# A fused attention and gated feed-forward kernel: new order and filler in the first batch, V projected behind the sums in the second

## The chip, the cores and the metric

The kernel runs on one core of a Trainium2 chip. Times are device microseconds of one execution; a span is the same execution from its first to its last instruction, some 1.8 us shorter. An execution counts as fast when it is within 1.5% of the fastest of its kernel.

PE is the matrix engine (PEld its weight loads), DVE the vector engine, ACT the scalar engine, POOL is GpSimd, SP the engine that issues the other transfers.

## The reference

```python
# batch 8, heads 8, sequence 1024, head size 64; E and F project the sequence to 64
k_proj = einsum('ks,bhsd->bhkd', E, k);  v_proj = einsum('ks,bhsd->bhkd', F, v)
scores = q @ k_proj.T / 8
attn = exp(scores - max);  attn = attn / (sum(attn) + 1e-9)
x = (attn @ v_proj) as [8192 tokens, 512]
out = (sigmoid(x @ w_gate) * (x @ w_val)) @ w_out          # 512 -> 1536 -> 512
```

## The kernel before

Nearly all of the time is the feed-forward part, "dense work": for each half batch of 512 tokens twelve pairs of matmul groups (gate into one bank of PSUM, value into another), then output projections. The attention of the next batch is put between them, in numbered slots. Only the first batch's attention has nothing to hide behind. It is done in half units with filler matmuls in the gaps, whose results nobody reads:

```python
def busy(n):                       # filler: keeps PE going
    for _ in range(n):
        mm(FB[3], bank[FB[3]][:, 0:P], ident[:, :], ident[:, :], ["ident"])
# ...
start_loads(); constants(); project_consts()
busy(6)
k_part(0); busy(3); turn_k(whole, 0); busy(6); k_part(1); busy(3)   # K: project, keep, turn
qt(0, ("DVE", "ACT")); turn_k(whole, 1)                             # Q turned on PE
sc(0)                                                               # first scores and exp
qt(1, ("DVE", "DVE")); busy(6)
den(0)                                                              # first sums, reciprocal, split
sc(1)                                                               # second scores and exp
busy(4); v_part(0); den(1)
bc(0); busy(4); xo(0); busy(6)                                      # spread, attention output -> xT
v_part(1); bc(1)
load_q(1); load_k(1); load_v(1)                                     # issued by POOL
# ... then dense work; xo(1) behind its first group
```

The order of the calls is the order on each engine. `whole` is a fixed list of the PSUM banks that these calls take; whoever uses a bank again waits for its last reader. After the sums, DVE takes the reciprocal and splits it into two bf16 parts, which the "spread" matmuls bring to all partitions:

```python
dve(reciprocal(rden, bank))                    # L593 here, L783 in the second batch
dve(tensor_copy(rhi, rden))                    # L594: cast to bf16
dve(scalar_tensor_tensor(rhl, rhi, -1, rden))  # L596: the rest
```

The second batch (b == 1) has the same parts in slots 12 to 24:

```python
return [k_alone, lambda: turn_k(att), v_alone, lambda: sc(0), lambda: sc(1),
        lambda: (den(), rec(0, ...)), lambda: rec(1, ...), lambda: rec(2, ...), lambda: rec(3, ...),
        split, lambda: bc(0), lambda: bc(1), lambda: xo(0), lambda: xo(1)]
spots = (12, 13, 14, 15, 16, 17, 18, 19, 20, 20, 21, 22, 23, 24)
```

The softmax here doesn't subtract the row's maximum and nothing guards it: scores larger than these inputs give would overflow.

Of the kernel before, what the change touches and what calls it, by code (L numbers as in the profile page):

```python
# [118 lines left out]
def bass_linformer_attn__then__ffn_glu_sigmoid_kernel(  # L119
# [18 lines left out]
    with contextlib.ExitStack() as es:  # L138
# [52 lines left out]
        class Ring:  # L191
# [8 lines left out]
        A0, A1, A2, A3 = AB  # L200
        F0, F1, F2, F3 = FB
        whole = Ring(
            (A0, A1, A2, A3, F0)
            + (A0, A1, F1, F2, A2)
            + (A3, F0, F1)
            + (A0, A1, A3, F0)
            + (A2, F2, A0, A1, F1)
            + (A3, A2, A0, A1, A3, A2)
        )
        ffn, att = Ring(FB), Ring(AB)  # L210

        def mm(b, o, lhsT, rhs, r, start=True, stop=True, tp=None, tr=False):
            kw = {}
            if tp is not None:
                kw["tile_position"] = tp
            if tr:
                kw["is_transpose"] = True
            else:
                kw["start"], kw["stop"] = start, stop
            return add("PE", lambda e: e.matmul(o, lhsT, rhs, **kw), r=r, x=[("bank", b)])  # L220
# [5 lines left out]
        def dve(fn, r, w, b=None):  # L226
            x = [] if b is None else [("bank", b)]
            return add("DVE", fn, r=r, w=w, x=x)
# [218 lines left out]
        def busy(n):  # L447
            for _ in range(n):
                mm(FB[3], bank[FB[3]][:, 0:P], ident[:, :], ident[:, :], ["ident"])
# [47 lines left out]
        def turn_k(ring, R=None):  # L497
            bk = ring.next()
            ob = bank[bk][:, :].bitcast(BF16)
            rs = range(NR)[pairs(R)]  # L500
            for n, r in enumerate(rs):
                for g in range(2):
                    mm(
                        bk,
                        ob[64 * g : 64 * g + 64, n * P : (n + 1) * P],
                        kp[:, r, :],
                        ident[:, :],
                        [("kp", r // 2), "ident"],
                        tr=True,
                        tp=(0, 64 * g),  # L510
                    )
            act(
                kpD[:, 2 * rs[0] : 2 * rs[-1] + 2, :].rearrange("p h c -> p (h c)"),
                ob[:, 0 : P * len(rs)],
                [],
                [("kpD", x) for x in both(R)],
                b=bk,
            )
# [153 lines left out]
        def attention(b):  # L672
# [60 lines left out]
            def sc(r2):  # L733
                for r in (2 * r2, 2 * r2 + 1):
                    bks = [att.next(), att.next()]
                    for c in range(2):
                        h = 2 * r + c
                        for g in range(2):
                            gg, oo = slice(64 * g, 64 * g + 64), 64 * (g ^ c)
                            mm(  # L740
                                bks[g],
                                bank[bks[g]][oo : oo + 64, :],
                                kpD[gg, h, :],
                                qT[s][gg, h, :],
                                [("kpD", r // 2), ("qT", s, r)],
                                tp=(64 * g, oo),
                            )
                    for g in range(2):
                        act(
                            eT[:, 2 * r + g, :],  # L750
                            bank[bks[g]][:, :],
                            [],
                            [("eT", 2 * r + g)],
                            b=bks[g],
                            func=AF.Exp,
                            scale=SCALE,
                        )

            def den():
                bk = att.next()  # L760
                for rnd in range(2):
                    for j in range(4):
                        n = 4 * rnd + j
                        mm(
                            bk,
                            bank[bk][32 * j : 32 * j + 32, :],
                            dsel[:, n % 2, rnd, :],
                            eT[:, n, :],
                            [("dsel", n % 2), ("eT", n)],
                            start=(rnd == 0),  # L770
                            stop=(rnd == 1),
                            tp=(0, 32 * j),
                        )
                if b == 1:
                    den_bank.append(bk)
                else:
                    for c in range(4):
                        rec(c, bk)

            def rec(c, bk):  # L780
                cc = slice(c * P, (c + 1) * P)
                dve(
                    lambda e: e.reciprocal(rden[:, cc], bank[bk][:, cc]),  # L783
                    [],
                    [("rden", c, R) for R in range(2)],
                    b=bk,
                )
# [77 lines left out]
            if b == 1:  # L865
                return [
                    k_alone,
                    lambda: turn_k(att),
                    v_alone,
                    lambda: sc(0),  # L870
                    lambda: sc(1),
                    lambda: (den(), rec(0, den_bank[0])),
                    lambda: rec(1, den_bank[0]),
                    lambda: rec(2, den_bank[0]),
                    lambda: rec(3, den_bank[0]),
                    split,
                    lambda: bc(0),
                    lambda: bc(1),
                    lambda: xo(0),
                    lambda: xo(1),  # L880
                ]
# [104 lines left out]
        start_loads()  # L986
        constants()
        project_consts()
        busy(6)
        qt, sc, den, bc, xo = half_unit(0, whole)  # L990

        def k_part(R):
# [7 lines left out]
            keep_v(bks, 0, ["ACT"] * 4, R)  # L1000

        k_part(0)
        busy(3)
        turn_k(whole, 0)
        busy(6)
        k_part(1)
        busy(3)
        qt(0, ("DVE", "ACT"))
# [1 line left out]
        sc(0)  # L1010
        qt(1, ("DVE", "DVE"))
        busy(6)
        den(0)
        sc(1)
        busy(4)
        v_part(0)
        den(1)
        bc(0)
        busy(4)
        xo(0)  # L1020
        busy(6)
        v_part(1)
        bc(1)
        load_q(1)
# [18 lines left out]
        for b in range(B):  # L1043
            todo = []
            for blk in (2 * b, 2 * b + 1):
                ms = [[m] for m in range(NF)]
                if blk <= 1:
                    ms = [[0, 1]] + ms[2:]
                if blk == 1:
                    gaps = {11: [0, 1, 2, 3]}  # L1050
                else:
                    gaps = {2: [0], 5: [1], 8: [2], 11: [3]}
                for m in ms:
                    if len(m) == 2:
                        todo.append(
                            lambda blk=blk: first_pair(blk, None if blk else lambda: xo(1))
                        )
                    else:
                        todo.append(lambda blk=blk, m=m[0]: mstep(blk, m))
                    if blk >= 1:  # L1060
                        for tt in gaps.get(m[-1], ()):
                            todo.append(lambda blk=blk, tt=tt: oproj(blk - 1, tt, ffn.next()))
            at = {}

            def put(i, fn):
                at.setdefault(i, []).append(fn)

            if b == 0:
                qt2, sc2, den2, bc2, xo2 = half_unit(1, att)
                put(4, lambda: (qt2(0, ("DVE", "ACT")), qt2(1, ("DVE", "ACT"))))  # L1070
                put(5, lambda: (sc2(0), sc2(1)))
                put(6, den2)
                put(8, lambda: (bc2(0), bc2(1)))
                put(9, lambda: (xo2(0), xo2(1)))
                spots = (12, 13, 14, 15, 16, 17, 18, 19, 20, 20, 21, 22, 23, 24)
            else:
                spots = (3, 6, 10, 13, 16, 16, 20, 23, 26, 29)
            if b + 1 < B:
                for i, fn in zip(spots, attention(b + 1)):
                    put(i, fn)  # L1080
            def load_next(n):
                load_k(n)
                load_q(n)
                load_v(n)

            if b == 0:
                put(16, lambda: load_next(2))
                put(24, lambda: transpose_q(2))
            else:
                if b + 2 < B:  # L1090
                    put(4, lambda b=b: load_next(b + 2))
                    put(20, lambda b=b: transpose_q(b + 2))
            for i, slot in enumerate(todo):
                slot()
                for fn in at.get(i, ()):
                    fn()
            assert max(at, default=0) < len(todo)
# [33 lines left out]
```

## Time and profile before

| | before |
|---|---|
| median of 3 executions | 568.17 us (567.77 to 569.35) |
| the execution that was traced | 569.20 us, span 567.4 us |
| PE busy | 550.5 of 567.4 us, 97% |
| waits of PE after its start | 1.2 us for rhl (second batch), 1.4 us for xT in all, 1.0 us for K |
| first Q half landed, clock at full rate, dense work begins | 13.2, 14.15, 22.4 us |

The 22.4 us are the first weight load (22.37), since the record of the first matmul is missing from this trace; one of the waits for xT is overstated by that.

With PE at 97% the places to look at are PE's waits, and for each wait the engine that ends it. The lines are in the prediction. One mark is used below: the start of the third pair of groups of dense work ("third pair").

### The profile page before, as it was taken

The numbers are of one execution on the slowest core, as the hardware profiler recorded it, in microseconds if no ns is written. First come the engines' busy times: TensorE is split into PE (matmuls) and PEld (weight loads), VectorE is DVE, ScalarE is ACT, GpSimd is POOL, SyncE is SP. The second block draws the span as 40 slices with busy tenths as digits, with TensorE's granted clock in tenths as the row PEclk, the third lists the DMA queues.
The fourth block names the chain that finished last, engine by engine and source line by source line (L and its number), as shares of the span: only waits on it lengthen the run. The fifth ranks groups of instructions, "written<-read, shape, count | busy, mean of one in ns | idle before, by whom it ended". The sixth has DMA issues, their size and how long they took to land.

```text
span 567.4 us, 7629 instructions
## 1 busy us (share of the span) xinstructions
PE 550.5 (97%) x2963; PEld 247.0 (44%) x3018; DVE 249.5 (44%) x397; ACT 177.4 (31%) x314; POOL 107.2 (19%) x148
## 2 busy tenths in 40 slices
PE   5899999999999999999999999999999999999998
PEld 4444434444444444444444444444444444444444
DVE  4544464353623545235443256334462354633332
ACT  2644632432143322352223422243214332222220
POOL 9400201007200080002600054000700007000000
PEclk9999999999999999999999999999999999999999
DMA  9999999936944059512677046560601001010112
GB/s 162 198 201 201 140 212 167 208 79 115 146 84 96 21 113 183 93 47 62 117 141 121 24 105 107 121 103 37 114 18 48 37 22 39 37 37 20 38 38 92
DMA packets 76564, 56.00 MB, mean 99 GB/s; under 512 B 34704, under 2 KB 68240, under 8 KB 76528
## 3 DMA queue, kind: packets, MB, share of 16 engines
q0 software_dynamic: 33984, 29.89, 34.8%
q1 hardware_dynamic: 42544, 25.63, 18.1%
q8 instruction: 23, 0.38, 0.3%
q14 instruction: 13, 0.11, 0.1%
HBM read 60.29 MB, written 16.78 MB: 136 GB/s over the span
## 4 chain that ended last, share of the span: by engine, by line
PE 95%; DVE 1%; DMA 1%; issue 1%; ACT 0%; POOL 0%; DVEq 0%; POOLq 0%
PE pF L220 88%; PE pA L220 7%; DMA KV<-in_k_dram 1%; DVE xT L645 1%; DVE hT L940 0%; DVE rden L783 0%; DVE rhl L794 0%; ACT qT L224 0%; DVE rhi L792 0%; POOL quad L313 0%; DVE ost L971 0%; DVEq L102 0%; POOLq L1116 0%
## 5 line engine op out<-in xcount | busy, mean ns | idle before, releaser
L940 DVE SCALAR_TENSOR_TENSOR hT<-sig,pF 128x512 bf16<-128x512 f32 x192 | 130.8, 685 | 200.0 <-PE pF L220 145.1
L224 ACT ACTIVATE sig<-pF 128x512 f32<-128x512 f32 x192 | 114.4, 599 | 318.3 <-PE pF L220 315.9
L220 PE MATMUL pF<-xT,wV 128*128 128x512 bf16 x753 | 196.2, 379 | 1.1 <-DVE hT L940 0.3
L220 PE MATMUL pF<-xT,wG 128*128 128x512 bf16 x746 | 194.4, 379 | 2.8 <-issue 1.3
L220 PE MATMUL pF<-wO,hT 128*128 128x512 bf16 (+2 forms) x762 | 173.9, 376 | 1.5 <-issue 0.8
L220 PEld LDWEIGHTS pF<-wO,hT 128*128 128x128 bf16 x780 | 74.7, 98 | 92.6 <-issue 6.2
L220 PEld LDWEIGHTS pF<-xT,wV 128*128 128x128 bf16 x768 | 75.1, 98 | 91.1 <-DVE hT L940 0.8
L220 PEld LDWEIGHTS pF<-xT,wG 128*128 128x128 bf16 x768 | 72.2, 98 | 95.3 <-issue 12.3
L829 POOL PARTITION_BROADCAST rb<-rrow x96 | 70.7, 798 | 217.1 <-DMA rrow<-rden 212.0
L971 DVE TENSOR_SCALAR ost<-pF 128x512 f32<-128x512 f32 (+1 forms) x65 | 44.4, 684 | 103.5 <-PE pF L220 103.4
L224 ACT ACTIVATE eT<-pA 128x512 bf16<-128x512 f32 x63 | 32.7, 606 | 8.4 <-PE pA L220 8.4
L854 DVE TENSOR_TENSOR xT<-pA,rb 128x512 bf16<-128x512 f32 x56 | 34.7, 682 | 0.0
L783 DVE RECIPROCAL rden<-pA 128x128 f32<-128x128 f32 x28 | 24.1, 916 | 0.0
L238 POOL DMA_DIRECT2D KV<-in_v_dram x9 | 7.8, 872 | 83.9 <-PE pF L220 83.9
L220 PE MATMUL pA<-KV,EFT 128*64 128x512 bf16 (+2 forms) x168 | 16.0, 332 | 1.0 <-DMA KV<-in_k_dram 1.0
L224 ACT ACTIVATE kpd<-pA 64x1024 bf16<-64x1024 f32 x6 | 6.1, 1017 | 28.3 <-PE pA L220 28.3
L238 POOL DMA_DIRECT2D KV<-in_k_dram x9 | 8.0, 889 | 32.3 <-PE pF L220 32.2
L220 PEld LDWEIGHTS pA<-KV,EFT 128*64 128x64 bf16 x168 | 8.3, 115 | 8.6 <-issue 3.4
L224 ACT ACTIVATE vpD<-pA 64x512 bf16<-64x512 f32 (+2 forms) x22 | 10.2, 465 | 2.2 <-PE pA L220 1.7
L220 PE MATMUL pA<-qT,kpD 64*64 64x512 bf16 (+1 forms) x140 | 10.4, 367 | 0.0
L220 PE MATMUL pA<-eT,vpD 64*64 64x512 bf16 (+1 forms) x140 | 10.4, 367 | 0.0
L238 POOL DMA_DIRECT2D Qb<-in_q_dram x11 | 9.4, 865 | 0.0
(69 smaller groups left out, 89.5 us busy)
## 6 DMA issues: line engine op xcount, KB each, us to landing
out_dram<-ost SPq DMA_DIRECT2D x63, 256.0 KB, 2.1
Qb<-in_q_dram POOLq DMA_DIRECT2D x7, 1024.0 KB, 15.6
KV<-in_k_dram POOLq DMA_DIRECT2D x7, 1024.0 KB, 11.0
KV<-in_v_dram POOLq DMA_DIRECT2D x7, 1024.0 KB, 10.5
wO<-in_moe_w_out_dram POOLq DMA_DIRECT2D x1, 1536.0 KB, 12.0
wG<-in_moe_w_gate_dram POOLq DMA_DIRECT2D x5, 256.0 KB, 18.4
wV<-in_moe_w_val_dram POOLq DMA_DIRECT2D x5, 256.0 KB, 19.0
KV<-in_k_dram POOLq DMA_DIRECT2D x2, 512.0 KB, 8.8
```

The source lines that it names most:

```text
L220: return add("PE", lambda e: e.matmul(o, lhsT, rhs, **kw), r=r, x=[("bank", b)])
L224: return add("ACT", lambda e: e.activation(o, i, func, scale=scale), r=r, w=w, x=x)
L238: add("POOL", lambda e: e.dma_start(o, i), r=r, w=w, dma=sem)
L645: lambda e, g=g, o=o: e.tensor_tensor(o, bank[bks[g]][:, :].rearrange("p (r c) -> p r c", r=2), rb[:, 2 * R + g, :].rearrange("p (r c) -> ...
L783: lambda e: e.reciprocal(rden[:, cc], bank[bk][:, cc]),
L829: lambda e, n=n, i=2 * rnd + c, j=j, parts=parts: e.partition_broadcast(rb[0:parts, n, :], rrow[32 * j : 32 * j + 1, i, :], channels=parts),
L854: lambda e, r=r, g=g, n=n, bk=bks[g]: e.tensor_tensor(xT[s][:, r, :, 256 * g : 256 * g + 256], bank[bk][:, :].rearrange("p (f c) -> p f c" ...
L940: lambda e: e.scalar_tensor_tensor(hT[blk % 2][:, m, :], sg[:, :], 1.0, bank[pv][:, :], ALU.add, ALU.mult,),
L971: lambda e, pb=pb, c0=c0, c1=c1: e.tensor_scalar(o[:, c0:c1], bank[pb][:, 0 : c1 - c0], 0.5, None, op0=ALU.mult),
```

## The change

The intent: turn PE's clock up earlier with more filler ahead of K, take the second scores out from behind the first sums, free the second spread of a busy bank, and give the second batch's reciprocals one slot more by moving V behind the sums.

```diff
         whole = Ring(
             (A0, A1, A2, A3, F0)
             + (A0, A1, F1, F2, A2)
-            + (A3, F0, F1)
-            + (A0, A1, A3, F0)
-            + (A2, F2, A0, A1, F1)
-            + (A3, A2, A0, A1, A3, A2)
+            + (A3, F0, A0, A1, F1)
+            + (A3, F0, A2)
+            + (F2, A0, A1, F1)
+            + (A3, A2, F2, A0, A3, A2)
         )
@@ second batch
-                    v_alone,
                     lambda: sc(0),
                     lambda: sc(1),
                     lambda: (den(), rec(0, den_bank[0])),
                     lambda: rec(1, den_bank[0]),
                     lambda: rec(2, den_bank[0]),
+                    v_alone,
                     lambda: rec(3, den_bank[0]),
@@ start
-        busy(6)
+        busy(18)
         k_part(0)
-        busy(3)
+        busy(4)
         turn_k(whole, 0)
-        busy(6)
+        busy(10)
@@
         busy(6)
+        sc(1)
         den(0)
-        sc(1)
@@
         xo(0)
-        busy(6)
+        busy(3)
@@
-                spots = (12, 13, 14, 15, 16, 17, 18, 19, 20, 20, 21, 22, 23, 24)
+                spots = (12, 13, 14, 15, 16, 17, 18, 18, 19, 19, 21, 22, 23, 24)
```

## The prediction

> **What bounds the kernel now.** I read the page first, then the waits of PE, then the timeline of PE and DVE around the two places that the change touches, then the landing times of the loads. The page says how much there is to win at all:
>
> ```profile
> span 567.4 us, 7629 instructions
> PE 550.5 (97%) x2963; PEld 247.0 (44%) x3018; DVE 249.5 (44%) x397; ACT 177.4 (31%) x314; POOL 107.2 (19%) x148
> PE   5899999999999999999999999999999999999998
> PE 95%; DVE 1%; DMA 1%; issue 1%; ACT 0%; POOL 0%; DVEq 0%; POOLq 0%
> ```
>
> PE is busy for 97% of the span, and the only slices below 90% are the first two and the last. 567.4 - 550.5 = 16.9 us are all that PE is idle. So no reordering can win over 3% unless it also makes matmuls shorter. The waits of PE, the whole span, tell where those idle times are:
>
> ```profile
> PE pA L220 <- DMA EF<-in_F_dram: 5.8, 1, 5.8
> PE pF L220 <- issue: 2.1, 13, 0.2
> PE pA L220 <- DVE rhl L794: 1.2, 1, 1.2
> PE pA L220 <- DMA KV<-in_k_dram: 1.0, 1, 1.0
> PE pF L220 <- DVE xT L645: 0.9, 3, 0.5
> PE pA L220 <- DVE xT L645: 0.5, 1, 0.5
> ```
>
> The columns are total us, times, longest. The 5.8 us at the start wait for E and F and are not touched. Two lines are what the change aims at: 1.2 us for rhl (L794, the second batch) and the waits for xT (L645, the first). The second batch in the timelines, PE then DVE:
>
> ```profile
> 72.88 1.03 PE L220 MATMUL pF<-xT,wV 128*128 128x512 bf16 x4
> 75.15 0.39 PE L220 MATMUL pA<-rhl,bsel 32*128 32x512 bf16 x4 [1.24 <-DVE rhl L794]
> ...
> 72.28 0.69 DVE L940 SCALAR_TENSOR_TENSOR hT<-sig,pF 128x512 bf16<-128x512 f32 x1 [0.17 <-PE pF L220]
> 72.89 0.95 DVE L783 RECIPROCAL rden<-pA 128x128 f32<-128x128 f32 x1
> 73.88 0.43 DVE L792 CAST rhi<-rden 128x512 bf16<-128x512 f32 x1
> 74.34 0.75 DVE L794 SCALAR_TENSOR_TENSOR rhl<-rhi,rows,rden 128x512 bf16<-128x512 bf16 x1
> ```
>
> The fourth reciprocal and the split run on DVE after a gate (72.28) and end at 75.09; the broadcast matmuls that need them could have begun at 73.84. And the start of the kernel:
>
> ```profile
> 13.89 0.43 DVE L549 COPY qT<-pA 128x512 bf16<-128x512 bf16 x1 [7.17 <-PE pA L220]
> 18.94 0.96 DVE L593 RECIPROCAL rden<-pA 64x128 f32<-64x128 f32 x1 [0.42 <-PE pA L220]
> 20.97 0.69 DVE L645 TENSOR_TENSOR xT<-pA,rb 128x512 bf16<-128x512 f32 x1
> 21.58 0.68 DVE L645 TENSOR_TENSOR xT<-pF,rb 128x512 bf16<-128x512 f32 x1
> ...
> L220 PE MATMUL pF<-KV,EFT x24: 219/314/316, 11.9 to 17.9; 128*64 128x128 bf16 x24
> ```
>
> Dense work (the gate and value matmuls) begins when xT is ready, at 22.4 us, and DVE's chain of sums, split and xT is what comes last. The last line (min/median/max ns) shows one matmul shape at two speeds, 314 ns early and 219 ns later. In the timeline, sixteen of them take 1.06 us at 9.35 and at 11.92, and 0.64 us at 20.32; the turn from slow to fast lies between 13.3 and 14.2 us. The row PEclk of the page reads 9 in every slice and does not show it.
>
> [...] 128-column matmuls start 107 ns apart early and 56 ns apart later[...]; this kernel waits by whole bank, and the trace shows it: the second spread waits 0.50 us for "DVE xT L645", a reader of the old contents of its bank A1, although its own data (rhl) are there at 20.94.
>
> **The change part by part.** Both kernels do the same useful work; only filler is added (18+4+10+3 in place of 6+3+6+6 at the four places changed, so 14 more on PE) and order moves.
>
> (a) Second batch. Slots are one pair of gate and value groups each, 1.73 us of PE (8 x 0.216). Before, V (16 matmuls, 0.89 us) comes after slot 14, scores after 15 and 16, sums after 17, reciprocals after 17 to 20, spread after 21. Now scores after 14 and 15, sums and first reciprocal after 16, V after 18, the fourth reciprocal and the split after 19, spread still after 21. The PE work ahead of the spread is the same, so PE gets there at 73.84 again in the old time frame (72.88 + 4 x 0.216 + 0.1 for the change of tile). When is rhl there? V's matmuls now end near 68.6; ACT copies vpD for 1.58 us (59.73 to 61.31 in the old trace), so until 70.2; then sigmoid 19, 0.6, to 70.8; gate 19 on DVE, 0.69, to 71.5; reciprocal 0.95 (its row), 72.45; cast 0.43; split 0.75; ready at about 73.65. That is 0.2 us before PE asks. So the wait goes whole: 75.15 - 73.84 = **1.3 us**, of which 0.2 us of margin is thin. Gates 20 and 21 come 1 us later on DVE, but the four matmuls groups behind them are output projections of the half batch before, whose inputs are long there.
>
> (b) First batch, the clock. The 12 extra fillers run in the wait for K: 18 x 0.107 = 1.93 us from 7.5, so to 9.43 where K was begun at 9.35; a cost of 0.1 us that later slack takes up (0.2 us of waiting before the second K half at 11.92). They make PE busy without a gap from about 7.3 on[...]. What gets faster on the path: the first Q half lands at 13.2 (issued at 2.98, 10.2 us to landing), so nothing before that moves the end. From there the eight transposes of Q take 0.62 in place of 1.03: **0.4 us**.
>
> (c) First batch, second scores ahead of the first sums. They stood behind sums that waited for exp (16.09 to 16.90). Now they follow the copies of qT directly: with (b), exp of the second scores ends near 17.5 in place of 18.44. V's first half lands at 17.0 and is not hurried; the second sums come at 17.5 to 17.9. DVE finishes the first split at 18.1, the second reciprocal runs 18.15 to 19.1, second split done at 20.05, xT from 20.1 to 21.4. Dense work begins near 21.5 against 22.4: **0.9 us**, (b) included.
>
> (d) Other banks for the second spread (F2, A0 for A0, A1). Their readers end by 20.6, so it runs at 20.4 to 20.7, not at 21.7. The second spread's copies then start after vpD (V's second half lands at 19.65, copies to about 21.6), and the second xT ends near 23.7, against 24.79. So the matmuls that need all of xT start near 23.8 in place of 24.93: **1.1 us** for (b), (c) and (d) together. The new bank F2 is also the third group's of the first pair; it is asked for near 22.7 and read out by 22.2, so no wait.
>
> Sum: 1.3 + 1.1 = 2.4 us if both come whole.
>
> **The rivals.** 1. The saved time turns into a wait for a load. For: loads fill the first 60 us (DMA row at 9). Against, by landing times: first weights 20.3 to 22.4 for 21.5 to 24.3; wV of the fourth chunk 33.1 against 35.3 less 1.1; transposed Q of batch 1 in four parts from 55.6 to 58.7, while the first scores now ask near 57.5 for two parts landed by 56.4 and the second near 60 for the rest; wO lands at 71.3 and is asked for near 73. The margins are 1 to 2 us: this could eat some tenths. Total near 566.5. 2. The clock does not turn earlier[...]. Then sc(1) still moves, by 0.5 us, and dense work by 0.3 to 0.4: total gain 1.3 + 0.4 = 1.7, 566.5. 3. V's copies on ACT (1.58 us) delay the gate that the last reciprocal stands behind, by more than I count; margin 0.2 us. If they cost 0.5 more, the second batch gains only 1.0. 4. ACT becomes the bound of the start: its queue of exp, vpD and rb is in one order, and V's landings fix two points of it. Then the gain of (b) to (d) is 0.5, total 566.4.
>
> **Range and chances.** 568.17 - 2.4 = 565.8. Weighing the rivals (each some tenths, all one way) I take 2.1 off: 566.1. The runs before spread over 1.6 us (567.77 to 569.35)[...]; the low end, 565.0, needs both gains whole and a good draw; the high end, 567.5, is a gain under 0.7. 2% would be 11.4 us, more than two thirds of PE's whole idle time, so faster or slower by that much would need something I don't see.
>
> **What would show each step.** (a): the wait "DVE rhl L794" of 1.2 gone from PE's waits, rhl done before slot 21 ends. (b): matmuls of 219 ns for the second K half at 11.9. (c): first xT matmul near 21.5. (d): no wait of PE for "DVE xT L645" ahead of the second spread. From 100 us on all must be the old trace, moved earlier by one constant amount. It is wrong if that amount is under 0.7 us, if PE waits for KV, qT, w or wO, or if anything after 100 us changes.

The forecast's sum came to 2.4 us, 1.3 for (a) and 1.1 for (b) to (d), of which I took 2.1. That PE's clock would turn up ahead of Q's transposes in the changed kernel, on which the 0.4 us of (b) within the 1.1 rest, was an assumption of mine, and no trace shows that filler does it. The two lengths are measured: eight transposes took 1.03 us in the first trace (13.24 us), 0.62 us in the changed kernel's (13.37 us).

## The result, and the profile after

The changed kernel took 567.51 us in the median of four executions (567.09 to 568.35); the kernel before, 568.76 (567.77 to 569.41). The ratio is 0.9981, 95% interval 0.9959 to 1.0003: the same within 2%, about 1.1 us less. Ratios here and below are the mean time of one kernel's fast runs over that of the other's, so not quite the ratio of the medians quoted. The median lies 0.01 us outside the predicted range. The class was right, and the saving about half of the 2.1 us forecast.

The page of the changed kernel, its span, PE's busy time and the granted clock by slices:

```profile
span 566.5 us, 7713 instructions
PE 556.0 (98%) x3032; PEld 247.5 (44%) x3032; DVE 248.8 (44%) x397; ACT 177.6 (31%) x314; POOL 107.4 (19%) x148
PEclk9899999999999999999999999999999999999999
```

PE's busy time is 5.5 us higher at a shorter span. That is no work added: of the 69 matmul records more in this trace only 14 are fillers, and the other 55 were missing from the first trace. The 8 in PEclk is new. The waits of PE over the whole span (total us, times, longest us):

```profile
PE pA L220 <- DVE dsel L398: 5.6, 1, 5.6
PE pF L220 <- DVE xT L645: 0.9, 2, 0.7
PE pF L220 <- DVE rhl L596: 0.4, 1, 0.4
PE pA L220 <- DMA Qb<-in_q_dram: 0.4, 1, 0.4
PE pF L220 <- DVE hT L940: 0.3, 1, 0.3
```

The 1.2 us for "DVE rhl L794" are gone. The timelines of the second batch, PE and then DVE (start us, duration us), show how narrowly:

```profile
73.34 1.03 PE L220 MATMUL pF<-xT,wV 128*128 128x512 bf16 x4
74.30 0.39 PE L220 MATMUL pA<-rhl,bsel 32*128 32x512 bf16 x4
```

```profile
71.39 0.69 DVE L940 SCALAR_TENSOR_TENSOR hT<-sig,pF 128x512 bf16<-128x512 f32 x1 [1.64 <-ACT sig L224]
71.99 0.95 DVE L783 RECIPROCAL rden<-pA 128x128 f32<-128x128 f32 x1
73.44 0.75 DVE L794 SCALAR_TENSOR_TENSOR rhl<-rhi,rows,rden 128x512 bf16<-128x512 bf16 x1
```

The split ends at 74.19 and PE asks at 74.30. The spread follows the value group at once (0.10 us after 73.34 + 4 x 0.216), where PE idled 1.24 us between the two before.

The start holds the surprise. PE in the timeline of the changed kernel, then one line of the kernel before:

```profile
21.64 0.98 PE L220 MATMUL pF<-xT,wG 128*128 128x512 bf16 x2 [0.69 <-DVE xT L645]
...
24.80 0.76 PE L220 MATMUL pF<-xT,wV 128*128 128x512 bf16 x2
25.39 0.59 PE L220 MATMUL pF<-xT,wG 128*128 128x512 bf16 x2
...
27.12 1.03 PE L220 MATMUL pF<-xT,wG 128*128 128x512 bf16 x4
```

```profile
26.66 1.03 PE L220 MATMUL pF<-xT,wG 128*128 128x512 bf16 x4
```

Dense work begins at 21.64, 0.76 us earlier than before. Yet the third pair begins at 27.12, 0.46 us *later*. Two matmuls that take 0.59 us from 25.39 on took 0.98 to 1.06 us before that. The table by stretches says why (columns: stretch, its length, then busy us of PE, PEld, DVE, ACT, POOL with counts, granted clock, DMA share, GB/s):

```profile
18.24:21.65 3.41, 2.32 (x48) 1.51 (x49) 3.12 (x6) 2.73 (x9) 2.29 (x3) 1.00 1.42 195
21.65:25.06 3.41, 3.41 (x15) 1.01 (x16) 1.29 (x2) 1.34 (x3) 0.00 (x0) 0.51 1.45 195
25.06:28.47 3.41, 3.41 (x17) 1.52 (x16) 1.38 (x2) 1.48 (x3) 0.00 (x0) 0.99 1.45 196
```

For 3.41 us from 21.7 on the clock was granted at half rate (0.51 in the second row), just as dense work began. That is the 8 in PEclk, and the mean clock of this execution is 0.997. Of the other three executions none has a mean below 1.0. So a drop was one cause to test, and not the only one.

### The profile page after: what moved, and what is told of

Same layout as the page of the kernel before. It is cut to its first block, busy times and chain, and to the rows that moved or that the text cites. A ratio compares the mean times of both kernels' runs of the same rounds, so it can differ in the third digit from the quotient of the medians.

```text
span 566.5 us, 7713 instructions
## 1 busy us (share of the span) xinstructions
PE 556.0 (98%) x3032; PEld 247.5 (44%) x3032; DVE 248.8 (44%) x397; ACT 177.6 (31%) x314; POOL 107.4 (19%) x148
## 4 chain that ended last, share of the span: by engine, by line
PE 95%; DMA 2%; DVE 1%; POOL 1%; ACT 0%; issue 0%; POOLq 0%
PE pF L220 89%; PE pA L220 7%; DMA KV<-in_v_dram 2%; DVE xT L645 1%; POOL KV L238 0%; POOL Qb L238 0%; DVE hT L940 0%; ACT rb L224 0%; ACT vpD L224 0%; POOL quad L313 0%; DVE ost L971 0%; POOLq L1116 0%
## 5 line engine op out<-in xcount | busy, mean ns | idle before, releaser
L220 PE MATMUL pF<-xT,wG 128*128 128x512 bf16 x768 | 199.0, 381 | 0.9 <-DVE xT L645 0.9
L220 PE MATMUL pF<-xT,wV 128*128 128x512 bf16 x768 | 198.4, 380 | 0.3 <-DVE hT L940 0.3
L220 PE MATMUL pF<-wO,hT 128*128 128x512 bf16 (+1 forms) x780 | 175.8, 376 | 0.0
L224 ACT ACTIVATE vpD<-pA 64x512 bf16<-64x512 f32 (+2 forms) x22 | 10.3, 466 | 2.5 <-PE pA L220 2.1
```

The source lines that it names most:

```text
L220: return add("PE", lambda e: e.matmul(o, lhsT, rhs, **kw), r=r, x=[("bank", b)])
L224: return add("ACT", lambda e: e.activation(o, i, func, scale=scale), r=r, w=w, x=x)
```

## The experiments

Fifteen runs were made beside the kernel before, all correct; three of them (`before_b`, `start_b`, `after_b`) repeat a kernel for a second trace. "Third pair" is the start of its first matmul; in the expectations I had read it from its first weight load, 0.2 us earlier. A "drop" is an execution with a mean clock of 0.997 or less: one stretch of 3.41 us at half rate, as in the changed kernel's trace, is 0.003 of the span.

### The two halves of the change alone

`v_only` is the kernel before with the new second batch:

```diff
-                    v_alone,
                     lambda: sc(0),
...
+                    v_alone,
                     lambda: rec(3, den_bank[0]),
-spots = (12, 13, 14, 15, 16, 17, 18, 19, 20, 20, 21, 22, 23, 24)
+spots = (12, 13, 14, 15, 16, 17, 18, 18, 19, 19, 21, 22, 23, 24)
```

> The kernel before with only the second batch's part of the change (V behind the sums, new slots); its start is the old one. Theory (the second batch gives its whole wait, the start gives little because the clock drops again): 1.2 to 1.3 us less than before, ratio near 0.9978, so nearly all that the whole change gave (1.25 us between medians); PE's wait for DVE rhl L794 gone, the start of the trace as before up to the draw of the clock. Rival (the second batch's gain is taken back later and the start is what gained): under 0.5 us less than before.

Measured: 567.96 against 568.71 us, ratio 0.9979 (0.9966 to 0.9993), 1.2 us less. The wait for L794 is gone.

`start_only` is the changed kernel with these lines put back as they were.

> The changed kernel with the second batch's part undone: only the start is new. Theory: executions fall in two groups. Where the granted clock drops after 21.6 us (mean clock below 1.0) the span is that of before or up to 0.5 us longer; where it doesn't drop, some 0.8 to 1.0 us shorter. Mean gain 0 to 0.6 us. Rival (the start gains its predicted 1.1 us in every execution and something later takes it back): a gain of 1.0 us or more in all, with the wait DVE rhl L794 back at 1.2 us.

Measured: 568.52 us, ratio 0.9996 (0.9981 to 1.001), 0.2 us less. The spans fall in two groups, as expected: three at 565.9 us, three at 567.4 to 567.6. But all six have a mean clock of 1.0, so my reason for the two groups was wrong. The kernel before has the same two groups at the same places: of 44 executions beside these experiments, 20 had spans up to 566.1 us and 17 of 567.3 or more.

What follows can be put exactly. From the third pair to the end of the span takes 540.7 us in every trace with the old second batch (567.4 - 26.66 before; 565.9 - 25.15 in `start_only`) and 539.4 us with the new one (566.5 - 27.12 changed; 566.1 - 26.68 in `v_only`), except in `best` (below), where it takes 540.3 (566.2 - 25.89). The second batch's part gives 1.3 us, and only in that one trace does a later wait take most of it back. Nearly all that went missing is ahead of the third pair.

### Is the drop caused by an idle PE?

`fill_gap` puts filler into the wait ahead of dense work.

```diff
         v_part(1)
         bc(1)
+        busy(10)
```

> The changed kernel with 10 more filler matmuls behind the second spread, in the 0.69 us in which PE waits for xT before dense work (20.95 to 21.64); they take about 0.56 us and move nothing on the path. Theory (the clock drops because the window from 18.2 to 21.65 was too idle): no execution has a mean clock under 1.0, granted clock 1.00 in all windows after 20 us, span near 565.2 in most executions, 0.3 to 0.8 us less than the changed kernel on average. Rival ([...] idle PE has no part): drops as often as in the changed kernel, mean time the same. Second rival (the filler comes into the way of dense work): 0.2 to 0.5 us longer.

Measured: 567.90 us, ratio 0.9977 (0.9964 to 0.9989). No execution dropped. But four of six had spans of 566.1 to 566.2 us at full clock, so I had expected too much of it. In its trace:

```profile
18.20:21.60 3.40, 3.11 (x60) 2.07 (x59) 2.49 (x5) 2.52 (x8) 2.33 (x3) 1.00 1.44 194
21.60:25.00 3.40, 3.21 (x22) 1.24 (x17) 1.56 (x3) 1.46 (x4) 0.00 (x0) 1.00 1.46 199
```

PE is busy for 3.11 of 3.40 us where it was for 2.32 in the changed kernel, and the clock stays. But it also stays in traces without this filler that are about as idle there. The drop at 21.71 us begins three times its own length of 3.41 us after the turn of the clock at 11.47, so the counts here are in windows of that length from the turn on; that other executions keep to such windows is not shown. In them PE is busy for 2.38 us in the changed kernel's window ahead of the drop (18.30 to 21.71), and for 2.44 us in `old_banks` (17.95 to 21.36) and 2.42 in `after_b` (18.92 to 22.34), where no drop follows. Nor does one follow windows with 2.27 us in `v1_late` (16.45 to 19.86) and 2.24 in `stt_old_filler` (8.65 to 12.06). Over all experiments, counting every execution:

| kernels | executions | with a drop |
|---|---|---|
| old start (before, v_only, before_b, before_stt) | 57 | 1 |
| new start or most of it, no filler in the gap | 52 | 13 |
| the same with filler in the gap (fill_gap, best) | 11 | 0 |
| v1_late (below), where PE waits 1.8 us for V | 6 | 4 |

So the new start brings the drop with it; it did so on each of the four chips. That idle PE is the cause is not shown. `fill_gap` ran on a chip on which the new start without filler had a drop in 1 of 12 executions only, so its 0 of 6 says little, and the 0 of 5 of `best` and the 4 of 6 of `v1_late` each stand beside 3 of 12. What a drop costs: `start_b` (below) has the same loads as the changed kernel to within 0.3 us and no drop; its dense work begins at 21.53 and the third pair at 25.78. So 27.12 - 25.78 less the 0.11 us of later beginning, 1.2 us.

### Two draws of each start

> The kernel before once more, for a second trace: its executions fall at 565.8 to 566.8 us and at 567.4 to 567.6 us, and the trace that I have is of the slower kind (first Q half landed at 13.2 us, clock at full rate from 14.15 us, dense work from 22.4 us). Theory (the prediction's saving at the start was measured from a slow draw: an execution of the old kernel whose loads land early or whose clock turns early has it already): a trace of a span under 566.3 us shows Q landed near 12.1 us or the clock turned before 12 us, and dense work beginning near 21.0 us. Rival (the two kinds differ later than the start): dense work begins at 22.4 us again and the 1.5 us are found after it. If the span is 567.4 us the trace tells nothing new.

A draw is one traced execution, with the landing times and the clock that it happened to get. `before_b` is the kernel before, once more. This execution was of the quick kind (565.9 us). PE in its timeline:

```profile
12.08 0.62 PE L220 MATMUL pA<-ident,Qb 128*128 128x128 bf16 x8 [0.41 <-DMA Qb<-in_q_dram]
...
19.47 0.64 PE L220 MATMUL pA<-KV,EFT 128*64 128x128 bf16 x16 [0.65 <-DMA KV<-in_v_dram]
20.66 0.59 PE L220 MATMUL pF<-xT,wG 128*128 128x512 bf16 x2 [0.22 <-DVE xT L645]
...
25.20 1.03 PE L220 MATMUL pF<-xT,wG 128*128 128x512 bf16 x4
```

The first Q half has landed at 12.04 us, 1.15 us earlier than in the first trace, and the transposes of Q take 0.62 us, not 1.03. The *old* start here waits for Q, waits 0.65 us for V's second half, and begins the third pair at 25.20.

> The kernel with only the start changed, once more: the trace that I have is of its faster kind (565.9 us, Q landed at 12.15 us, dense work from 20.9 us); three of six executions took 567.4 to 567.6 us at a full mean clock, and why is open. Theory (loads that land a microsecond later carry the whole start with them): a slow execution shows Q landed near 13.2 us, dense work begun near 21.7 us and no drop of the clock, and the rest of the 1.5 us in waits between 22 and 60 us. Rival (the late kind is a clock that turns late): Q landed near 12.1 us but full rate only from 14 us on. If the span is 565.9 us the trace tells nothing new.

`start_b`, the new start alone with late loads (Q at 13.21 us, full rate from 10.3 us) and no drop: third pair at 25.78. The span was 566.5 us, a third kind. So neither theory of the expectation was met in full: a late load alone does not give 567.4 us.

Putting the draws side by side (landing of Q's first and V's second half, full rate from, third pair; the turn to full rate is read from the matmuls, 314 ns of one shape ahead of it and 219 ns behind):

| trace | start | Q, V | full rate | third pair |
|---|---|---|---|---|
| before | old | 13.19, 19.63 | 14.15 | 26.66 |
| v_only | old | 13.02, 19.44 | 14.43 | 26.68 |
| before_b | old | 12.04, 19.43 | before 9 | 25.20 |
| start_b | new | 13.21, 19.66 | 10.31 | 25.78 |
| changed | new | 13.32, 19.94 | 11.47, a drop | 27.12 |
| start_only | new | 12.15, 19.16 | 11.37 | 25.15 |
| after_b | new | 12.25, 19.49 | 8.69 | 25.26 |

With late loads and a late clock in the old kernel's draw the new start is worth 0.88 us (26.66 to 25.78), of which 0.40 turn out below to be another matter. With early loads and an early clock it is worth nothing (25.20 to 25.15 or 25.26). With a drop it loses 0.46 us. The prediction was read from the first row.

### The parts of the start

`old_filler` goes back to busy(6), busy(3), busy(6) ahead of K and its turn.

> The changed kernel with the old filler counts ahead of K and its turn (6, 3, 6 for 18, 4, 10), all else changed. Theory (the filler turns the clock to full rate earlier, worth about 0.4 us on the path from 13.2 us on, but also fixes nothing of the later drop): the second K half's matmuls are of 314 ns in the trace, dense work begins near 22.0 in place of 21.64, 0.2 to 0.5 us longer than the changed kernel in executions without a drop. Rival (the early filler is what makes the clock drop later[...]): the drop is gone or rarer and the time the same as or less than that of the changed kernel.

Measured: 567.04 us, ratio 0.9973 (0.9957 to 0.9989), no slower than the changed kernel. My theory of 0.4 us for the filler is not borne out. In its trace the clock reached full rate at 11.25 us without it, K was taken up at 8.20 when it had landed at 7.87, and the third pair began at 24.92; in `fill_gap`, with 18 fillers ahead, K had landed at 8.02 and was taken up at 9.48. So in an early draw the filler stands in K's way.

`sums_first` puts den(0) ahead of sc(1) again (banks accordingly); `old_banks` gives the second spread A0 and A1 again.

> The changed kernel with only the order of the first batch undone (first sums ahead of the second scores; banks follow). As I predicted, the new order is worth 0.3 to 0.5 us on the path: exp of the second scores would end 0.4 us later in the trace and dense work begin 0.3 to 0.5 us later; time 0.3 to 0.5 us above the changed kernel's. Rival (the loads and DVE's first split set the start, and the order is hidden): the same time within 0.2 us, and the second reciprocal on DVE begins at the same distance from the landing of V's first half.

> The changed kernel with the old banks (A0, A1) for the second spread. As I predicted: PE waits 0.5 us for DVE xT L645 ahead of the spread again, the spread's copies on ACT stay behind vpD and so begin no later, and dense work begins at the same time; 0 to 0.4 us slower than the changed kernel. Rival (the banks were the start's gain): 0.5 us slower or more.

Measured on one chip, whose kernel before was mostly of the quick kind (median 567.78): `sums_first` 1.0006 (0.9993 to 1.0019), with a drop in three of five; `old_banks` 0.9991 (0.9978 to 1.0003), with a drop in two of six. The drops hide what each part is worth on average. The trace of `sums_first`, an early draw, has the third pair at 25.25, as `after_b` has: there the order is hidden. The trace of `old_banks`, a late draw, shows something that I had not thought of. DVE, then POOL:

```profile
18.09 0.71 DVE L594 CAST rhi<-rden 64x128 bf16<-64x128 f32 x1
...
20.21 0.34 DVE L594 CAST rhi<-rden 64x128 bf16<-64x128 f32 x1
20.97 0.69 DVE L645 TENSOR_TENSOR xT<-pA,rb 128x512 bf16<-128x512 f32 x1
```

```profile
17.73 1.02 POOL L238 DMA_DIRECT2D Qb<-in_q_dram  x1
19.47 1.03 POOL L238 DMA_DIRECT2D KV<-in_v_dram  x1
```

The same cast takes 0.22 us in the changed kernel's trace, 0.71 and 0.34 here, and both long ones end within 0.06 us of the end of a load issue on POOL (18.75 and 20.50). In the kernel before the second cast took 0.62 us (19.93 to 20.55) and in `v_only` 0.82 us (to 20.57). In all three xT begins at 20.97 to 21.00 us and the third pair at 26.65 to 26.68. POOL issues these loads at the same times in all traces but that of `issue_late`, to 0.1 us, so a held cast ties different starts to one time. It also has a part in the 0.88 us above. The second cast in the kernel before, then in `start_b`:

```profile
19.93 0.62 DVE L594 CAST rhi<-rden 64x128 bf16<-64x128 f32 x1
```

```profile
19.45 0.22 DVE L594 CAST rhi<-rden 64x128 bf16<-64x128 f32 x1
```

xT begins at 20.97 and at 20.09 us. Of the 0.88 us between them 0.48 are work moved up (the cast begins earlier) and 0.40 are the cast itself, which begins just ahead of the issue at 19.47 us in `start_b` and was not held up.

### Is it the cast?

`cast_stt` writes it as a two-input instruction with the same result; `before_stt` does so in the kernel before; `best` is `cast_stt` with `fill_gap`'s ten fillers. `issue_late` holds POOL's three issues until xT is written.

```diff
-dve(lambda e: e.tensor_copy(rhi[pp, 0:P], rden[pp, 0:P]), rd, ri)
+dve(lambda e: e.scalar_tensor_tensor(
+        rhi[pp, 0:P], rden[pp, 0:P], 1.0, rden[pp, 0:P], ALU.mult, ALU.max), rd, ri)
```

```diff
                 [("Q", s, hf, R) for hf in range(2) for R in range(2)],
                 f"Q{s}",
+                r=[("xT", 0, 0, 0, 0)] if b == 1 else (),
```

> The changed kernel with the cast of the first batch's split (rhi from rden, on DVE) written as a two-input instruction (rden times 1, max rden; the same result). In ten traces the cast took 0.22 us or up to 0.82 us, the long ones ending where one of GpSimd's load issues ends; where the second cast is long, the first xT begins at 20.97 to 21.00 us whatever the start was. Theory (the cast is held up by GpSimd's issues, and that pins slow executions at one time, 566.1 us of span with the new second batch): casts of 0.3 to 0.4 us in every trace, no cluster at 566.1 us, spans 564.5 to 565.4 us unless the clock drops, median 0.5 to 1.0 us below the changed kernel's 567.5. Rival (the slow kind is the loads that land late, and the cast is only its mark): spans of 566.1 us remain about as often, the median within 0.3 us of the changed kernel's.

> The changed kernel with GpSimd's last three load issues before the dense work (Q, K and V of the second batch, 17.7 to 20.5 us) held until the first xT is written; the cast is the old one. Theory (those issues hold up the cast): the second cast takes 0.22 us in every trace, no cluster at 566.1 us, median 0.4 to 0.9 us below the changed kernel's; the loads land no later than before, since the queue is behind anyway. Rival (late loads): spans of 566.1 us remain. If the later issue costs something, a wait for KV or qT appears near 45 to 60 us.

> The changed kernel with the two-input cast and the 10 fillers in the idle stretch ahead of dense work. Theory: neither the held-up cast nor a drop of the clock is left, so all executions have a mean clock that rounds to 1.0 and spans of 564.5 to 565.4 us: median near 566.8 us, 1.5 to 2.2 us below the kernel before and the narrowest spread of all. Rival: spread and median as the changed kernel's.

> The kernel before with only the cast written as a two-input instruction. Theory (its slow kind, spans of 567.4 us, has the second cast held up until 20.55 us): no cluster at 567.4; late loads and a late clock still show, so spans of 565.8 to 567.1 us, mean 0.2 to 0.5 us less than before. Rival (the slow kind comes from loads and clock alone): spans of 567.4 to 567.6 us as often as in the kernel before.

Measured on one chip (before 568.92 us):

| kernel | median | ratio (95%) | drops | spans |
|---|---|---|---|---|
| cast_stt | 566.89 | 0.9973 (0.9959 to 0.9987) | 1 of 6 | 564.5 to 565.5, with the drop 565.9 |
| issue_late | 567.58 | 0.9982 (0.9966 to 0.9997) | 2 of 6 | 564.6 to 566.0, with a drop 566.2, 566.3 |
| best | 567.45 | 0.9983 (0.9968 to 0.9997) | 0 of 5 | 565.2 to 566.2 |
| before_stt | 568.81 | 1.0004 (0.999 to 1.0019) | 0 of 6 | 566.0 to 567.5 |

The casts took 0.28 to 0.29 us in the traces of `cast_stt`, `best` and `before_stt`, and 0.22 to 0.23 in that of `issue_late`. In `cast_stt` the group at 566.1 us is gone, which fits the theory. But `before_stt` is no faster than the kernel before and still has two spans of 567.4 and 567.5: for the old kernel the theory failed and the rival fits better, though 2 of 6 against 5 of 11 in the kernel before is a small count, and its trace (566.5 us) is not of the slow kind, so what makes that kind without the cast is not shown. So a cast can take longer and end as a load issue of POOL ends, and the traces show it (0.62 us in the kernel before, 0.71 and 0.34 in `old_banks`, 0.22 twice in the changed kernel); that this is what makes the slow group of the new start is likely and not settled.

`issue_late` gained nothing (in the changed kernel's trace the three loads landed 26.7 to 37.2 us after their issue); its trace has a drop, and V's first half landed at 17.66 us where 15.8 to 16.1 was usual in early draws.

`best` was meant to beat all and didn't. Its profiled execution shows a new wait, in the second batch:

```profile
60.22 0.41 PE L220 MATMUL pA<-qT,kpD 64*64 64x512 bf16 x4
61.34 0.41 PE L220 MATMUL pA<-qT,kpD 64*64 64x512 bf16 x4 [0.71 <-DMA qT<-Qb]
```

The second scores, one slot earlier than before, ask at 60.6 us for the last part of the transposed Q, which landed at 61.2 in this execution and at 58.4 to 60.0 in all others. It is the first rival of the prediction, and a cost of the new slots; a wait of this size for it stands in one of 17 traces.

### The floor of the start

In `before_b`, `before_stt`, `sums_first`, `cast_stt` and `after_b`, old start and new, the third pair begins 5.77 or 5.78 us after V's second half lands; in `before_stt` the clock turned only at 14.78 us, and V still came last. Where V lands earlier something else comes last: 6.49 us after it in `old_filler` (V at 18.43). `v1_late` lets the first weights go ahead of it:

```diff
-            for R in range(2):
-                load_kv_heads(1, v, R)
+            load_kv_heads(1, v, 0)
             load_w(0, 0)
+            load_kv_heads(1, v, 1)
```

> The changed kernel with the first two weight loads issued ahead of V's second half, which so lands about 0.7 to 1.4 us later; nothing else waits for it before dense work. Theory (the landing of V's second half is the floor of the start): the third group of dense work begins 5.5 to 5.9 us after that landing in the trace, so near 25.8 to 26.8 us, and the fast executions (spans of 564.5 to 565.2 us) are gone; 0.5 to 1.2 us slower than the changed kernel on the same chip. Rival (the chain of DVE sets the start): third group at 24.9 to 25.7 us as before, time within 0.3 us.

> The changed kernel with the two-input cast and the old filler counts ahead of K. Theory (with the cast free the early filler only decides when the clock turns, and its 18 matmuls delay K in executions whose loads land early): spans of 564.3 to 566.0 us, the lowest below those of the changed kernel; median 0.4 to 1.0 us below the changed kernel's. Rival (the filler is needed to turn the clock in time): a group of spans at 565.8 us and above in half of the executions, median no better than the changed kernel's.

> The changed kernel once more, beside the two: spans of 564.5 to 566.6 us in the groups seen (early loads near 564.6, late loads near 565.2, cast held up or clock dropped 566.1 to 566.6), ratio to before 0.997 to 0.999 whatever the theory; its trace adds one draw with landing times, the turn of the clock and the two casts.

`v1_late`: 569.25 us, ratio 1.0008 (0.9992 to 1.0023), against 566.85 us, 0.9979 (0.9956 to 1.0003), of the changed kernel beside it (`after_b`). In its trace V's second half landed at 20.84 us:

```profile
20.88 0.64 PE L220 MATMUL pA<-KV,EFT 128*64 128x128 bf16 x16 [1.84 <-DMA KV<-in_v_dram]
```

```profile
19.86:23.27 3.41, 1.93 (x35) 1.04 (x36) 0.71 (x2) 1.54 (x5) 0.68 (x1) 1.00 1.45 196
23.27:26.69 3.42, 3.42 (x9) 1.25 (x10) 1.29 (x2) 0.63 (x2) 0.00 (x0) 0.50 1.45 196
```

PE idles 1.84 us for V, and then the clock drops. The two executions without a drop had spans of 566.4 and 566.5 us, where the changed kernel's best three have 564.5 to 564.7: 1.8 us later, for a landing that the two traces show 1.35 us later (20.84 against 19.49). In the trace the third pair begins at 27.91, 7.07 us after the landing, so some 5.9 without the 1.2 us of a drop. So a later landing moves the start by about its own delay, with a drop on top in four of six executions; an execution without a drop was not traced.

`stt_old_filler`: 567.42 us, 0.9976 (0.9959 to 0.9993), with the lowest span of all, 564.2, but also 567.4 (a drop) and 566.2. In the trace with 564.2 V has landed at 18.55 us, and the first dense matmul at 20.53 waits for its gate weights, which landed at 20.49, 0.15 us after xT was written (20.34): with V out of the way that load came last. `stt_old_filler` is not better than `after_b` beside it.

No kernel here is clearly faster than the changed one. `cast_stt` has the lowest ratio with `old_filler` (0.9973 each), and all intervals overlap.

## Why the prediction was right or wrong

**The bound and the class** were right: PE is busy for 98% of the span, nothing came near 2%.

**Step (a), the second batch, 1.3 us:** right to the tenth, and step by step: the third pair stands 0.46 us later than in the first trace, so rhl, done at 74.19, was done at 73.73 in the old time frame, for 73.65 predicted. From the third pair on 1.3 us are gone in every trace with it but one; the margin that I called thin was 0.1 us in place of 0.2. The exception is `best`, where the scores that now ask one slot earlier wait for the transposed Q and 0.9 of the 1.3 us are lost.

**Steps (b) to (d), the start, 1.1 us, failed: a mis-sized term of the sum.** Alone it measured 0.2 us (`start_only`). In the kind of draw that I had read it from it is 0.88 us without a drop, but only 0.48 of that are work moved up; 0.40 are a cast that was held up before and was not in `start_b`, which no step of mine had. And I took one trace for the kernel. That trace was of the slow kind: loads late, clock turned at 14.15 us, 569.20 us where the median was 568.17, as its own record said. An execution of the old kernel with early loads and an early clock already had all of it, because there V's second half is the floor, and the new start doesn't move that. I had the landing of V in the sum as a fact of the second xT, and didn't ask what the *old* start would do if the rest were earlier.

**Step (b) by itself,** the turn of the clock: right for the changed kernel's trace, where the second K half's sixteen matmuls took 0.64 us and not 1.06, with full rate from 11.47 us. The time that I had forecast for the turn rested on no trace, and full rate begins at another time in each execution (8.69 us in `after_b`, 14.43 in `v_only`). That the new filler is what turned the clock is not shown: with the old counts it turned at 11.25 us in `old_filler` and at 8.65 in `stt_old_filler`, and `old_filler` did as well.

**Step (c),** dense work at 21.5: 21.64 in the changed kernel, as predicted, but by luck: two errors cancel. I had the second reciprocal begin at 18.15 us, and it began at 18.57, since the first sums came no earlier (first reciprocal at 16.96, 16.94 before); and I had 0.95 us for the split behind it, the length that the held-up cast gave it, and it took 0.61 (19.56 to 20.17). What was missing is that the new start leaves PE idle for 0.69 us just ahead of dense work, and that the clock fell back right after it (to 0.51 for 3.41 us). I had thought of the clock's turning up and not of its way down.

**Step (d),** no wait for xT ahead of the second spread: right; the wait is gone in the changed kernel and back (0.41 us) in `old_banks`. The matmuls that need all of xT began at 24.06 us in `start_b`, for 23.8 predicted and 24.93 before, and at 25.39 in the changed kernel with its drop.

**The rivals.** The second (the clock) came nearest, in the wrong direction: it was not that the clock failed to turn up, but that it fell. The first (a transfer) showed once. The third and fourth didn't.

**Open.** Which of the start's edits brings the drop is not known, and neither is whether idle PE does. The drop stays with the old order (`sums_first`, 3 of 5), with the old banks (`old_banks`, 2 of 6) and with the old filler ahead of K (`old_filler` and `stt_old_filler`, 2 of 12); the one edit of the start that no run put back by itself is the shorter filler behind xo(0). Nor is it known why the loads land a microsecond earlier in some executions, with POOL's issues at the same times. The slow kind of the new start without a drop (567.4 us in `start_only`) was not caught in a trace; `old_banks`, whose third pair at 26.65 plus 540.7 makes 567.4, suggests the held cast.

## What to carry to other kernels

Before working out a saving of a microsecond, compare the traced execution's own time with the median, and take a second trace of the kernel before: here its own executions differ by 1.5 us, and a change that repairs what one slow draw shows is worth little in the others. Cut the span at a mark that both kernels share, and compare the two sides by themselves; that turned a noisy 1.2 us into 1.3 us that all traces but one show and 0.2 that are not certain. And when work is moved up ahead of a wait, look at how idle that leaves PE just before its dense work begins, and at the granted clock from there on (0.51 for 3.41 us in the changed kernel, after 2.38 of 3.41 us busy; the cause is not shown).

## What the traces show of the clock and of the cast

- The drop came after a stretch in which PE was busy for 2.38 of 3.41 us and its longest wait was 0.69 us (changed kernel), and after one with 1.93 us that begins within a wait of 1.84 us (`v1_late`). PE's busy share alone doesn't tell: in `v1_late` a window with 2.27 of 3.41 us was followed by no drop, and in `old_banks` 2.44 us with a wait of 0.91 by none. The two stretches at half rate in the tables above lasted 3.41 and 3.42 us (granted clock 0.50 to 0.51). Full rate began at another time in each execution: 8.69 us in `after_b`, 11.47 in the changed kernel, 14.43 in `v_only`.
- In `after_b` PE was busy for 3.02 of the 3.41 us up to the turn at 8.69 us (from 5.67 us on), first 1.74 us with nothing but transposes (of f32), then with filler. What turned the clock is not shown.
- The profile's granted clock reads 1.00 ahead of its first turn to full rate as well. In the kernel before, 128-column matmuls took 314 ns until about 14 us and 219 ns later, with a granted clock of 1.00 in both stretches; only a later drop is seen in it (0.51 in the changed kernel).
- The 64x128 cast took 0.22 us or up to 0.82 us (`v_only`), and 0.28 to 0.29 us in the two-input form. Long ones ended as a load issue of POOL ended: at 20.55 us in the kernel before (issue to 20.50), at 18.80 and 20.55 in `old_banks` (issues to 18.75 and 20.50). Not every cast that overlaps an issue is long. Those that began 0.06 and 0.18 us after an issue began (19.56 and 17.94 in the changed kernel, issues from 19.50 and 17.76) took 0.22 us, as did one 0.19 us after (17.92 in the kernel before, issue from 17.73). Those that began 0.36, 0.45 and 0.74 us after (18.09 in `old_banks`, 19.93 in the kernel before, 20.21 in `old_banks`, issues from 17.73, 19.48 and 19.47) took 0.71, 0.62 and 0.34 us. What holds the cast is not shown beyond that.
